# Attention followed by gated products on one core: places of two weight tiles, planner tables with PE's modes, and value products as one operation

## The chip, the cores and the metric
One NeuronCore of a Trainium2 chip runs the whole program. The metric is device microseconds of one execution; lower is better. TensorE is called PE below, VectorE DVE, ScalarE ACT, GpSimd POOL, SyncE SP.

## The reference
Inputs are q, k and v of 4 batches, 12 heads, 448 positions and 64 columns, and three weight matrices. In short:

```python
scores = q @ k.transpose / 8;  scores above the diagonal = -1e9
p = exp(scores - rowmax);  p = p / (p.sum + 1e-9)
x = (p @ v), heads side by side            # 1792 x 768
out = ((x @ w_a) * (x @ w_b)) @ w_out      # w_a, w_b 768 x 1536, w_out 1536 x 768
```

## The kernel before, in words
**Attention.** Two heads make a pair; there are 6 pairs a batch. For each pair `scores` (line 388) makes the lower triangle of q k in seven rows of blocks, r = 0 to 6, with 64x64 tiles of PE (line 413, four operations a pair: rows 6 and 5, row 0, rows 4 and 3, rows 2 and 1), takes each row's maximum on DVE (line 422) and its exponential on ACT (line 428), and scales by the inverse sum: on POOL for batches 0 and 1 (line 442), on ACT for batches 2 and 3 (line 441). `turn` (line 451) transposes p by PE in two turns of 8 (line 460), four to a PSUM bank (t0, t1), and copies each bank to SBUF on ACT or DVE. `values` (line 470) multiplies by v in 128x64 tiles of PE (line 478): four operations a pair, one for each quarter c of the keys, each of two products per head half; quarters 0 and 3 read the first turn, 1 and 2 the second. The result is x, split into a rounded part x_hi and a remainder x_lo (batches 0 and 1) or stored to HBM as x_keep (batches 2 and 3).

**Products.** Weights come in as 64-bit words, are made float32 in six steps (`convert_unit`, line 302) and split into w_hi (ACT) and w_lo (DVE). The tiles w_hi and w_lo have 18 slots of 128 x 128 each, 512 bytes a slot and partition. `products` (line 577) issues three matmuls of 448 columns for each 128-deep slice: w_hi by x_hi, w_hi by x_lo, w_lo by x_hi (line 581). Batches 0 and 1 go first: 24 units for a and b, 12 for the output. Batches 2 and 3 follow with seven products in place of eight (`seven`, line 658); `take_first` and `take_second` prepare their operands from x_keep. Attention of batches 2 and 3 is woven between the products of batches 0 and 1: one pair every 30 slices (`AT`, `attend`, line 762).

**Order.** Every operation is recorded with an engine and a duration (`Plan.op`, line 99), and its number is its urgency. `Plan.order` (line 123) then runs a clock per engine: at each step the engine that is free first takes the ready operation of the lowest number. When an operation is ready follows from the end of its predecessors plus `WAIT[engine][engine]` and `MARGIN`. What comes out is the order in which each engine executes; nothing is changed on the chip. Buffers are rings (`ring`, line 90): a new user of a slot waits for all users of the old one.

**Places.** Tiles are laid one behind the other in SBUF. Before, w_hi and w_lo start at 64 modulo 512 bytes in a partition, and the moving operands (x_hi, x_lo, g_hi, g_lo and the rooms of the second half) at 64 modulo 256, with slices of 1792 bytes, which is 7 times 256.

Of the kernel before, what the change touches and what calls it, by code (L numbers as in the profile page):

```python
# [79 lines left out]
class Plan:  # L80
# [18 lines left out]
    def op(self, engine, ns, fn, reads=(), writes=()):  # L99
# [21 lines left out]
        self.ops.append((engine, ns, fn, deps, self.soonest))  # L121

    def order(self):
# [16 lines left out]
        count = 0  # L140
        while count < n:
# [14 lines left out]
            if now[e]:  # L156
                i = now[e][0]
                limit = at + PATIENCE[e] * self.ops[i][1]
                first = [s for s in soon[e] if s[0] < limit and s[1] < i - GAP] if PATIENCE[e] else []
                if first:  # L160
                    s = min(first, key=lambda s: s[1])
                    soon[e].remove(s)
                    heapq.heapify(soon[e])
                    at, i = s
                else:
                    heapq.heappop(now[e])
            else:
                i = heapq.heappop(soon[e])[1]
# [7 lines left out]
            else:  # L176
                free[e] = end[i] = at + self.ops[i][1]
# [17 lines left out]
def pe_ns(n, passes=1):  # L195
    return max(passes * n / 2.4, 107.0) + 2.5
# [19 lines left out]
def causal_attention_then_gated_product(  # L216
# [39 lines left out]
    g_lo = const.tile([P, 2, HF, S], F32R, name="g_lo")  # L256
    w_keep = [dram.tile([P, UW], F32, name=f"w_keep{u}") for u in range(NU)]
# [44 lines left out]
    def convert_unit():  # L302
# [12 lines left out]
        plan.op("dve", 660, lambda: nc.vector.tensor_scalar(  # L315
            out=e.t, in0=high(), scalar1=0x7FF00000, scalar2=None, op0=ALU.bitwise_and), [t], [e])
        plan.op("dve", 660, lambda: nc.vector.tensor_scalar(
# [4 lines left out]
        plan.op("dve", 1030, lambda: nc.vector.scalar_tensor_tensor(  # L322
            out=r(), in0=m.t, scalar=2.0**32, in1=low(), op0=ALU.mult, op1=ALU.add), [m, t], [m])
        plan.op("dve", 1030, lambda: nc.vector.scalar_tensor_tensor(
            out=e.t, in0=high(), scalar=0x80000000, in1=e.t,
            op0=ALU.bitwise_and, op1=ALU.bitwise_or), [t, e], [e])
        plan.op("dve", 1030, lambda: nc.vector.scalar_tensor_tensor(  # L327
# [60 lines left out]
    def scores(b, hp):  # L388
        qk_t = qk.pop((b, hp))
        st = plan.ring("st", 2, None)  # L390
        st.tile = st_buf[nth[3] % 2]
# [7 lines left out]
        for part, tags in ((FIRST, ("s0", "s1")), (SECOND, ("m", "m") if b < 2 else ("t0", "t1"))):  # L399
            banks = [bank(tag, 3 if tag == "m" else 1) for tag in tags]  # L400
            at = {}
            for rs in part:
# [14 lines left out]
                plan.op("pe", pe_ns(D * (rs[0] + 1), 4) + 60, mm, [(qk_t, 0), (qk_t, 1)], [at[r][0] for r in rs])  # L417
            for r in [r for rs in part for r in rs]:
# [16 lines left out]
        plan.op("dve", 165, lambda: nc.vector.tensor_scalar_add(st.t[:, rc, 0:NR], st.t[:, sm, 0:NR], 1.0e-9),  # L435
                [(st, sm, r) for r in rows], [(st, rc, r) for r in rows])
        plan.op("dve", 170, lambda: nc.vector.reciprocal(st.t[:, rc, 0:NR], st.t[:, rc, 0:NR]), [], [(st, rc, r) for r in rows])
        for r in rows:
# [7 lines left out]
            ns = act_ns(D * (r + 1), False, 1) if NORM[b] == "act" else pool_ns(D * (r + 1))  # L446
# [23 lines left out]
    def values(b, hp, x):  # L470
        ps, vt = bank("pv"), v_of.pop((b, hp))
        parts = dict(pt)
        for c in range(4):
            n, (o, count) = next((n, g[1:]) for n in range(2) for g in groups[n] if g[0] == c)

            def mm(c=c, n=n, o=o, count=count):
                for j in range(2):
# [4 lines left out]
                return r  # L482
# [393 lines left out]
```

## Time and profile before

| | us |
|---|---|
| median of 3 runs (670.26 to 671.44) | 671.21 |
| the profiled execution | 670.64 |
| its span, first to last instruction | 668.9 |
| PE busy (3,956 matmuls) | 659.9 |
| DVE busy | 453.7 |
| ACT busy | 349.0 |
| POOL busy | 49.8 |

The span is cut below at 101.7 us, where the first long run of products begins, and at 387.1 us, where the last value products end. Durations of matmuls are modelled and overlap; how fast PE goes is read from the starts of instructions one behind the other.

### The profile page before, as it was taken

What the parts mean: (1) busy time and instruction counts of PE and PEld (TensorE: products, weight loads), DVE (VectorE), ACT (ScalarE), POOL (GpSimd) and SP (SyncE); (2) the same over time, 40 slices, a digit from 0 to 9 for tenths busy, and PEclk for the clock granted to TensorE, in tenths of its full rate; (3) what the DMA queues carried; (4) which work ended last, traced back from release to release, by engine and by line L of the source; (5) the groups of instructions that cost most, each with busy time, mean ns of one, the idle gap of its engine ahead of it and who ended that gap; (6) DMA issues with size and microseconds to landing.
All of it is one profiled execution on the core that took longest, in us unless ns stands there. A gap on an engine that the chain in (4) does not pass through costs nothing.

```text
span 668.9 us, 10897 instructions
## 1 busy us (share of the span) xinstructions
PE 659.9 (99%) x3956; PEld 559.8 (84%) x3956; DVE 453.7 (68%) x1005; ACT 349.0 (52%) x826; POOL 49.8 (7%) x104
## 2 busy tenths in 40 slices
PE   8999999999999999999999999999999999999997
PEld 6554469889888888888988989999999999999997
DVE  4778878888778567568768795588762237886431
ACT  5888746765675675675576742244432234443110
POOL 3546530000000000000000000000000000000000
PEclk9999999999999999999999999999999999999999
DMA  8535535666476665454432275212133232122532
GB/s 281 179 98 182 168 89 202 219 211 204 163 241 242 210 217 207 125 197 160 167 126 73 68 230 164 91 60 71 50 94 103 102 103 60 60 72 79 163 112 95
DMA packets 41717, 95.87 MB, mean 143 GB/s; under 512 B 4800, under 2 KB 27840, under 8 KB 41664
## 3 DMA queue, kind: packets, MB, share of 16 engines
q1 hardware_dynamic: 41664, 95.18, 43.3%
q8 instruction: 31, 0.51, 0.3%
q14 instruction: 22, 0.18, 0.1%
HBM read 67.24 MB, written 27.92 MB: 142 GB/s over the span
## 4 chain that ended last, share of the span: by engine, by line
PE 95%; POOL 3%; DVE 1%; POOLq 0%; issue 0%; ACT 0%
PE m L581 76%; PE t L460 7%; PE pv L478 5%; PE s L413 3%; POOL early L442 2%; PE t L413 2%; PE m L413 2%; POOL p L442 1%; PE fill L816 1%; POOLq L871 0%; DVE pt L272 0%; DVE p L422 0%; DVE w L327 0%; ACT w_hi L264 0%; DVE mid L280 0%
## 5 line engine op out<-in xcount | busy, mean ns | idle before, releaser
L581 PE MATMUL m<-x_hi,w_hi 128*128 128x448 f32 x432 | 161.2, 373 | 0.0
L581 PE MATMUL m<-x_hi,w_lo 128*128 128x448 f32 x432 | 157.9, 366 | 0.0
L581 PE MATMUL m<-x_lo,w_hi 128*128 128x448 f32 x432 | 157.8, 365 | 0.0
L280 DVE TENSOR_TENSOR w_lo<-w,w_hi 128x768 fp32r<-128x768 f32 (+1 forms) x84 | 66.0, 786 | 63.3 <-ACT w_hi L264 62.5
L581 PE MATMUL m<-g_hi,w_hi 128*128 128x448 f32 x288 | 106.1, 368 | 0.0
L581 PE MATMUL m<-g_hi,w_lo 128*128 128x448 f32 x288 | 105.3, 366 | 0.0
L581 PE MATMUL m<-g_lo,w_hi 128*128 128x448 f32 x288 | 105.3, 365 | 0.0
L264 ACT ACTIVATE w_hi<-w 128x768 fp32r<-128x768 f32 (+1 forms) x84 | 59.2, 705 | 71.0 <-PE m L581 49.3
L581 PEld LDWEIGHTS m<-x_hi,w_hi 128*128 128x128 f32 x432 | 81.3, 188 | 8.4 <-issue 1.7
L581 PEld LDWEIGHTS m<-x_hi,w_lo 128*128 128x128 f32 x432 | 81.1, 188 | 6.7
L581 PEld LDWEIGHTS m<-x_lo,w_hi 128*128 128x128 f32 x432 | 81.2, 188 | 6.1
L264 ACT ACTIVATE mid<-m 128x448 f32<-128x448 f32 x72 | 38.9, 540 | 90.4 <-PE m L581 76.8
L428 ACT ACTIVATE p<-p,st 128x384 f32<-128x384 f32 (+6 forms) x126 | 62.4, 497 | 23.8 <-DVE st L422 23.6
L280 DVE TENSOR_TENSOR mid<-m,acc 128x448 f32<-128x448 f32 x48 | 29.9, 624 | 46.3 <-PE m L581 45.6
L581 PEld LDWEIGHTS m<-g_hi,w_hi 128*128 128x128 f32 x288 | 54.1, 188 | 4.5
L581 PEld LDWEIGHTS m<-g_hi,w_lo 128*128 128x128 f32 x288 | 54.1, 188 | 4.4
L581 PEld LDWEIGHTS m<-g_lo,w_hi 128*128 128x128 f32 x288 | 54.1, 188 | 4.2
L264 ACT ACTIVATE pt<-t 128x512 f32<-128x512 f32 x72 | 40.6, 596 | 26.5 <-PE t L460 26.1
L478 PE MATMUL pv<-pt,v 128*64 128x448 f32 (+3 forms) x384 | 49.5, 389 | 0.0
L478 PEld LDWEIGHTS pv<-pt,v 128*64 128x64 f32 x384 | 24.5, 136 | 22.6 <-issue 11.5
L460 PE MATMUL t<-ident,p 128*128 128x128 f32 x180 | 38.8, 279 | 0.9 <-DVE pt L272 0.7
L280 DVE TENSOR_TENSOR mid<-m,mid 128x448 f32<-128x448 f32 x36 | 22.5, 625 | 23.5 <-PE m L581 23.2
(90 smaller groups left out, 999.2 us busy)
## 6 DMA issues: line engine op xcount, KB each, us to landing
w<-w SPq DMA_DIRECT2D x36, 768.0 KB, 4.5
w_keep<-w SPq DMA_DIRECT2D x36, 384.0 KB, 2.9
w<-w_keep SPq DMA_DIRECT2D x36, 384.0 KB, 3.1
raw<-qT SPq DMA_DIRECT2D x24, 224.0 KB, 2.6
raw<-kT SPq DMA_DIRECT2D x24, 224.0 KB, 3.1
o_keep<-mid SPq DMA_DIRECT2D x24, 224.0 KB, 2.0
acc<-o_keep SPq DMA_DIRECT2D x24, 224.0 KB, 2.7
out<-mid SPq DMA_DIRECT2D x24, 224.0 KB, 1.9
```

Source lines behind the costliest of these rows:

```text
L264: return nc.scalar.activation(o(), i(), AF.Copy)
L280: plan.op(engine, ns, lambda: e.tensor_tensor(out=o(), in0=a(), in1=b(), op=op), reads, writes)
L413: x = nc.tensor.matmul(at[r][0].t[to * D:(to + 1) * D, at[r][1]], q[:, r * D:(r + 1) * D], k[:, 0:D * (r + 1)], start=True, stop=True)
L428: return nc.scalar.activation(view(r), view(r), AF.Exp, bias=st.t[:, nm, r:r + 1], scale=-1.0, accum_out=st.t[:, sm, r:r + 1],)
L442: return nc.gpsimd.tensor_scalar(out=view(r), in0=view(r), scalar1=st.t[:, rc, r:r + 1], scalar2=1.0, op0=ALU.mult, op1=ALU.mult)
L460: return nc.tensor.matmul(t.t[:, P * i:P * (i + 1)], p.t[:, PO[r] + P * c:PO[r] + P * (c + 1)], swapped if r % 2 else ident, is_transpose= ...
L478: r = nc.tensor.matmul(ps.t[j * D:(j + 1) * D, 128 * c:S], vt.t[:, c, j, :], parts[n].t[:, j, o:o + count, :].rearrange("p i d -> p (i d)" ...
L581: r = nc.tensor.matmul(ps.t[:, :S], a[:, i, :], x(), start=first and n == 0, stop=last and n == 2, skip_group_check=part)
L816: plan.filler = lambda: nc.tensor.matmul(fill[:, 0:P], warm, warm, start=True, stop=True)
```

## The change
It has four parts. The two weight tiles move behind the other constant tiles, each behind a spacer of 192 bytes, so that w_hi starts at 0 modulo 512 and w_lo at 192 modulo 256. The planner's waits and durations are set anew, and PE's operations carry a mode: "q" for scores, "c" for values, "f" for all others. A change of mode is charged `SWITCH` nanoseconds on the plan's clock, and where the most urgent ready operation of PE is of another mode, PE takes the first ready one of the mode at hand if its number is less than `NEAR` = 100 beyond. The four operations of `values` become one, which reads both turns' copies and both parts of v. The ring of small tiles st, which hold a pair's maxima and sums, goes from 2 to 4 slots.

```diff
 WAIT = {
-    "pe": {"pe": 0, "act": 200, "dve": 200, "pool": 270, "sp": 200},
-    "act": {"pe": 260, "act": 140, "dve": 145, "pool": 205, "sp": 150},
-    "dve": {"pe": 290, "act": 130, "dve": 130, "pool": 205, "sp": 150},
-    "pool": {"pe": 260, "act": 320, "dve": 320, "pool": 200, "sp": 250},
+    "pe": {"pe": 0, "act": 180, "dve": 210, "pool": 270, "sp": 200},
+    "act": {"pe": 160, "act": 140, "dve": 110, "pool": 205, "sp": 150},
+    "dve": {"pe": 150, "act": 100, "dve": 130, "pool": 210, "sp": 150},
+    "pool": {"pe": 80, "act": 200, "dve": 200, "pool": 200, "sp": 250},
...
-MARGIN = 60
+MARGIN = 20
+NEAR = 100
+SWITCH = {"fq": 95, "qf": 160, "qc": 220, "cq": 220, "fc": 150, "cf": 107}
...
             if now[e]:
                 i = now[e][0]
+                if e == "pe" and self.ops[i][5] != mode:
+                    alike = [j for j in now[e] if self.ops[j][5] == mode and j < i + NEAR]
+                    if alike:
+                        i = min(alike)
...
-                free[e] = end[i] = at + self.ops[i][1]
+                ns = self.ops[i][1]
+                if e == "pe":
+                    ns += SWITCH.get(mode + self.ops[i][5], 0)
+                    mode = self.ops[i][5]
+                free[e] = end[i] = at + ns
...
-    st_buf = [sbuf.tile([P, 3, 8], F32, tag=f"st{i}", name=f"st{i}") for i in range(2)]
+    st_all = sbuf.tile([P, 4, 28], F32, tag="st", name="st")
+    st_buf = [st_all[:, i, 0:24].rearrange("p (n r) -> p n r", n=3) for i in range(4)]
...
-    w_hi = const.tile([P, 18, P], F32R, name="w_hi")
-    w_lo = const.tile([P, 18, P], F32R, name="w_lo")
     v_buf = [const.tile([P, 4, 2, D], F32, name=f"v{i}") for i in range(NVB)]
...
     g_lo = const.tile([P, 2, HF, S], F32R, name="g_lo")
+    const.tile([P, 48], F32, name="space")
+    w_hi = const.tile([P, 18, P], F32R, name="w_hi")
+    const.tile([P, 48], F32, name="space_2")
+    w_lo = const.tile([P, 18, P], F32R, name="w_lo")
...
-        plan.op("dve", 660, lambda: nc.vector.tensor_scalar(
+        plan.op("dve", 470, lambda: nc.vector.tensor_scalar(
...
-        plan.op("dve", 1030, lambda: nc.vector.scalar_tensor_tensor(
+        plan.op("dve", 900, lambda: nc.vector.scalar_tensor_tensor(
...
-    st = plan.ring("st", 2, None)
+    st = plan.ring("st", 4, None)
...
-                plan.op("pe", pe_ns(D * (rs[0] + 1), 4) + 60, mm, [(qk_t, 0), (qk_t, 1)], [at[r][0] for r in rs])
+                plan.op("pe", pe_ns(D * (rs[0] + 1), 4), mm, [(qk_t, 0), (qk_t, 1)], [at[r][0] for r in rs], "q")
...
-                plan.op("dve", dve_ns(n) + 70, negmax, [at[r][0], "mask"], [(p, r), (st, nm, r)])
-                plan.op("act", act_ns(n, False, 3), exp, [(st, nm, r)], [(p, r), (st, sm, r)])
+                plan.op("dve", dve_ns(n) + 10, negmax, [at[r][0], "mask"], [(p, r), (st, nm, r)])
+                plan.op("act", act_ns(n, False, 2), exp, [(st, nm, r)], [(p, r), (st, sm, r)])
...
-            ns = act_ns(D * (r + 1), False, 1) if NORM[b] == "act" else pool_ns(D * (r + 1))
+            ns = act_ns(D * (r + 1)) if NORM[b] == "act" else pool_ns(D * (r + 1))
...
-        for c in range(4):
-            n, (o, count) = next((n, g[1:]) for n in range(2) for g in groups[n] if g[0] == c)
-
-            def mm(c=c, n=n, o=o, count=count):
+        def mm():
+            for c in range(4):
+                n, (o, count) = next((n, g[1:]) for n in range(2) for g in groups[n] if g[0] == c)
                 for j in range(2):
...
-            plan.op("pe", pe_ns(S - 128 * c, 4) + 60, mm,
-                    [(vt, 1 if c == 3 else 0), (parts[n], 0), (parts[n], 1)], [ps])
+        plan.op("pe", sum(pe_ns(S - 128 * c, 4) for c in range(4)), mm,
+                [(vt, 0), (vt, 1), *((parts[n], h) for n in range(2) for h in range(2))], [ps], "c")
```

## Rows read from the trace of the kernel before

**Rows 1.** The page: PE's sum, granted clock by slice, and the chain's shares.
```profile
PE 659.9 (99%) x3956; PEld 559.8 (84%) x3956; DVE 453.7 (68%) x1005; ACT 349.0 (52%) x826; POOL 49.8 (7%) x104
...
PEclk9999999999999999999999999999999999999999
...
PE 95%; POOL 3%; DVE 1%; POOLq 0%; issue 0%; ACT 0%
```

**Rows 2.** Busy time (and count) by stage: all engines, then PE and weight loads of line 581.
```profile
0.00:101.70 101.70, 96.47 (x820) 56.91 (x820) 75.19 (x270) 71.56 (x220) 49.79 (x104) 1.00 0.52 167
...
387.10:668.90 281.80, 278.04 (x1371) 257.38 (x1371) 1.00 0.32 101
...
0.00:668.90 668.90, 515.87 (x2484) 463.33 (x2484) 1.00 0.44 143
```

**Rows 3.** Timeline, products stage: start us, duration us, engine, what, count.
```profile
387.01 0.47 PE L581 MATMUL m<-g_hi,w_hi 128*128 128x448 f32 x1
...
599.92 0.36 PE L581 MATMUL m<-x_hi,w_hi 128*128 128x448 f32 x1
...
600.32 0.37 PE L581 MATMUL m<-x_hi,w_lo 128*128 128x448 f32 x1
600.53 0.36 PE L581 MATMUL m<-x_hi,w_hi 128*128 128x448 f32 x1
...
601.13 0.36 PE L581 MATMUL m<-w_x,w_hi 128*128 128x448 f32 x1
...
664.77 0.37 PE L581 MATMUL m<-g_hi,w_lo 128*128 128x448 f32 x1
```

**Rows 4.** Timeline of PE, attention stage, values of one pair and scores of another.
```profile
43.29 0.97 PE L478 MATMUL pv<-pt,v 128*64 128x448 f32 x4
44.20 0.33 PE L460 MATMUL t<-ident,p 128*128 128x128 f32 x1
...
45.59 0.33 PE L460 MATMUL t<-swapped,p 128*128 128x128 f32 x1
45.75 0.27 PE L460 MATMUL t<-ident,p 128*128 128x128 f32 x1
45.86 0.27 PE L460 MATMUL t<-swapped,p 128*128 128x128 f32 x1
46.06 0.97 PE L413 MATMUL s<-raw 64*64 64x448 f32 x8
46.96 0.33 PE L460 MATMUL t<-ident,p 128*128 128x128 f32 x1
...
47.33 0.27 PE L413 MATMUL s<-raw 64*64 64x64 f32 x2
```

**Rows 5.** Timeline of PE, mixed stage, one pair.
```profile
120.30 0.36 PE L581 MATMUL m<-x_hi,w_lo 128*128 128x448 f32 x1
120.59 1.02 PE L413 MATMUL s<-raw 64*64 64x448 f32 x10
...
122.47 1.95 PE L478 MATMUL pv<-pt,v 128*64 128x448 f32 x16
124.34 0.47 PE L581 MATMUL m<-x_hi,w_hi 128*128 128x448 f32 x1
```

**Rows 6.** Timeline of PE, attention stage: a transpose that waits for a copy.
```profile
15.87 0.27 PE L460 MATMUL t<-swapped,p 128*128 128x128 f32 x1
16.82 0.44 PE L460 MATMUL t<-ident,p 128*128 128x128 f32 x2 [0.68 <-DVE pt L272]
```

**Rows 7.** Timeline of DVE, then of PE, where the second half begins.
```profile
402.56 0.62 DVE L280 TENSOR_TENSOR w_x<-raw,pt_x 128x448 fp32r<-128x448 f32 x1
...
424.21 0.36 PE L581 MATMUL m<-x_hi,w_hi 128*128 128x448 f32 x1
```

**Rows 8.** What PE waited for to 101.7 us: sum us, times, longest us.
```profile
PE t L460 <- POOL early L442: 2.2, 4, 0.7
PE t L460 <- POOL p L442: 1.0, 3, 0.6
```

More of the change, by code (lines that the diff above doesn't have):

```diff
@@ L97, in ring, with op @@
         return slots[i]
-    def op(self, engine, ns, fn, reads=(), writes=()):
+    def op(self, engine, ns, fn, reads=(), writes=(), mode="f"):
         i, deps = len(self.ops), set()
@@ L120, in op @@
         deps.discard(i)
-        self.ops.append((engine, ns, fn, deps, self.soonest))
+        self.ops.append((engine, ns, fn, deps, self.soonest, mode))
     def order(self):
@@ L139, in order @@
         out = []
-        count = 0
+        count, mode = 0, "f"
         while count < n:
@@ L165, in order @@
                 else:
-                    heapq.heappop(now[e])
+                    now[e].remove(i)
+                    heapq.heapify(now[e])
             else:
@@ L313, in r @@
             return m.t.bitcast(F32)
-        plan.op("dve", 660, lambda: nc.vector.tensor_scalar(
+        plan.op("dve", 470, lambda: nc.vector.tensor_scalar(
             out=e.t, in0=high(), scalar1=0x7FF00000, scalar2=None, op0=ALU.bitwise_and), [t], [e])
-        plan.op("dve", 660, lambda: nc.vector.tensor_scalar(
+        plan.op("dve", 470, lambda: nc.vector.tensor_scalar(
             out=m.t, in0=high(), scalar1=0x000FFFFF, scalar2=0x00100000,
@@ L321, in convert_unit @@
             e.t, e.t, AF.Copy, bias=-896.0 * 2**23, scale=8.0), [e], [e])
-        plan.op("dve", 1030, lambda: nc.vector.scalar_tensor_tensor(
+        plan.op("dve", 900, lambda: nc.vector.scalar_tensor_tensor(
             out=r(), in0=m.t, scalar=2.0**32, in1=low(), op0=ALU.mult, op1=ALU.add), [m, t], [m])
-        plan.op("dve", 1030, lambda: nc.vector.scalar_tensor_tensor(
+        plan.op("dve", 900, lambda: nc.vector.scalar_tensor_tensor(
             out=e.t, in0=high(), scalar=0x80000000, in1=e.t,
             op0=ALU.bitwise_and, op1=ALU.bitwise_or), [t, e], [e])
-        plan.op("dve", 1030, lambda: nc.vector.scalar_tensor_tensor(
+        plan.op("dve", 900, lambda: nc.vector.scalar_tensor_tensor(
             out=wt.t, in0=r(), scalar=2.0**-52, in1=e.t.bitcast(F32),
@@ L389, in scores @@
         qk_t = qk.pop((b, hp))
-        st = plan.ring("st", 2, None)
-        st.tile = st_buf[nth[3] % 2]
+        st = plan.ring("st", 4, None)
+        st.tile = st_buf[nth[3] % 4]
         nth[3] += 1
@@ L430, in exp @@
                     )
-                plan.op("dve", dve_ns(n) + 70, negmax, [at[r][0], "mask"], [(p, r), (st, nm, r)])
-                plan.op("act", act_ns(n, False, 3), exp, [(st, nm, r)], [(p, r), (st, sm, r)])
+                plan.op("dve", dve_ns(n) + 10, negmax, [at[r][0], "mask"], [(p, r), (st, nm, r)])
+                plan.op("act", act_ns(n, False, 2), exp, [(st, nm, r)], [(p, r), (st, sm, r)])
         rows = range(NR)
-        plan.op("dve", 165, lambda: nc.vector.tensor_scalar_add(st.t[:, rc, 0:NR], st.t[:, sm, 0:NR], 1.0e-9),
+        plan.op("dve", 76, lambda: nc.vector.tensor_scalar_add(st.t[:, rc, 0:NR], st.t[:, sm, 0:NR], 1.0e-9),
                 [(st, sm, r) for r in rows], [(st, rc, r) for r in rows])
-        plan.op("dve", 170, lambda: nc.vector.reciprocal(st.t[:, rc, 0:NR], st.t[:, rc, 0:NR]), [], [(st, rc, r) for r in rows])
+        plan.op("dve", 122, lambda: nc.vector.reciprocal(st.t[:, rc, 0:NR], st.t[:, rc, 0:NR]), [], [(st, rc, r) for r in rows])
         for r in rows:
```

2 lines of the change are left out of this document (1 added, 1 removed).

## The prediction

> **What bounds the kernel now.** Four views, in this order. The page's sums come first: TensorE (PE) is busy 659.9 us of a span of 668.9, and the clock granted to it is at its upper level (2.4 GHz) in all forty slices [rows 1]. A busy PE is not by itself PE at its peak, so the chain of waits is next: 95% of the path that ended last is PE, and POOL has 3% [rows 1]. Third, the span cut in three [rows 2]: an attention stage up to 101.7 us (VectorE, DVE, 75.2 us busy, ScalarE, ACT, 71.6), a mixed stage up to 387.1 us with attention of batches 2 and 3 between products, and a stage of products alone. Last the timeline of PE, to see the pace inside each stage.
>
> In the products stage nothing waits. Its 1,371 matmuls [rows 2] start from 387.01 to 664.77 us [rows 3]: 277.76 / 1,370 = 0.2027 us each. 448 columns at 2.4 GHz are 0.1867 us, so each costs 0.016 us more than its columns. All 2,484 products [rows 2] therefore hold 2,484 x 0.2027 = 503.5 us, three quarters of the span, and only two things shorten the rest: fewer matmuls, which the change doesn't bring, or a shorter step.
>
> In the attention stage PE goes to and fro between three kinds of work: transposes and products (f), score products of 64x64 tiles (q), value products of 128x64 tiles (c). The reader is to see in [rows 4] that the value products of one pair fall into two stretches with a transpose between, and that transposes break the scores of one pair as well; in [rows 5], from the mixed stage, both lie in one stretch each. By the whole timeline of PE to 101.7 us I count 31 stretches of q for 13 pairs and 23 of c for 12 pairs, 18 and 11 more than one a pair.
>
> **The price of going to and fro.** Values: whole, from 122.47 to 124.34 = 1.87 us [rows 5]; broken, from 43.29 to 45.59 = 2.30 with one transpose in it [rows 4]. A transpose among transposes takes 0.11 (45.75 to 45.86) [rows 4], so the break costs 2.30 - 1.87 - 0.11 = 0.32. The transposes' side of such a break is the two between scores (46.96 to 47.33), which take 0.37 and not 0.22: 0.15 of it [rows 4]. The other half is the way back into the tiled mode to the tiles, which scores pay as values do. I take 0.30 us for a further round trip, of values or of scores.
>
> **Value products as one operation.** The instructions stay (16 matmuls a pair); three waits and three places where the planner may put other work go. All 11 breaks go: 11 x 0.30 = 3.3 us. What it adds is a wait: the first quarter now also waits for the copies of the second turn. Behind the waiting matmul nothing on PE can pass, and the split of the result into x (ACT, DVE) comes later, which nobody needs before the products. The price of one such wait when nothing lies between: last transpose at 15.87, then DVE's copy out of the bank, and the next transpose into it at 16.82 [rows 6]; 0.95 - 0.11 = 0.84 us. Over 12 pairs the ends are 0 and 10.1 us. I take 1.0, near the lower end, because scores of the next pair, which need none of these copies, can lie between: as they do at 46.06 behind three transposes [rows 4].
>
> **PE's mode in the planner.** It stays with the kind of work at hand while an operation of that kind, ahead of or less than 100 numbers behind the most urgent one, is ready. Score products of one pair need no other engine's work between them, so most of the 18 further stretches can go; the PSUM banks that wait for VectorE's reads hold some. I take 13 of 18: 13 x 0.30 = 3.9 us (ends 0 and 18 x 0.30 = 5.4). In the mixed stage each pair has one stretch of each already [rows 5], so nothing is gained. There the rule lets products go ahead of ready scores, for up to 100 numbers. By the code a pair's share of the stage is 30 product operations, 35 that bring weights in and results out, and 57 of attention, 122 numbers in (387.1 - 101.7) / 12 = 23.8 us, so 100 are about 20 us. Values of the last pair feed the second half; its preparation ends on DVE at 402.56 + 0.62 and PE reads the first of it at 424.21 [rows 7]: 21 us of cover. I cost it at nothing; beyond the cover it costs a us for each us.
>
> **Tables and st.** Waits and durations change the plan's guesses, not the work. PE waits for POOL 3.2 us in the attention stage as the trace names it [rows 8], so better guesses are worth 0 to 3.2 there, and nothing later, where PE has no wait; an order that is rebuilt can lose as much. I take 0; what hides any other shift is the queue of ready work ahead of PE. Two more st slots take away a wait of DVE for POOL's norms two pairs back, off PE's path: 0, and the same 3.2 if PE's waits come from there.
>
> **The places of w_hi and w_lo.** All tiles that PE reads start now at 64 modulo 256 bytes and step by multiples of 256, so no row shows any other phase. Slices of x lie in turn at 64 and 320 modulo 512, yet two slices in turn take 0.61 and 0.60 us for their three products (599.92, 600.53, 601.13) [rows 3]: a step of 256 does nothing. So bounds: at best a product takes its columns alone, 0.016 x 2,484 = 39.7 us less. Nearer is how close the value products come to their columns: 1,024 columns in four passes at 2.4 GHz are 1.707 us of their 1.87 [rows 5]; a way out of a mode costs 0.09 of that (transpose to scores, 45.86 to 46.06, 0.20 in place of 0.11 [rows 4]), and 0.07 over eight steps leaves 0.009 each. By that a product could take 0.196: 0.0067 x 2,484 = 16.6 us less. The last product ahead of a switch, which has no weight load beside it, takes 120.30 to 120.59 = 0.29 [rows 5], 0.20 without the way out: 0.0027 x 2,484 = 6.7 us less. On the other side, a single start told to a hundredth can lie 0.21 behind the one before (600.32 to 600.53) [rows 3]; 0.21 throughout is 0.0073 x 2,484 = 18 us more. I take 0, the row that is there. The Trainium skill has a rule against this part (TensorE: Matmul & The Clock Gate, Step-by-step: what each phase is for): PE has two SBUF read ports, so that loading weights steals nothing from a running matmul. By it the places change nothing and the sum stays; that a product with a load beside it takes 0.203 and one without 0.20 doesn't settle it.
>
> **Sum.** Profiled execution 670.64 us (span 668.9 and 1.7 around it). -3.3 - 3.9 + 1.0 = -6.2: 664.4. The median of the runs is 0.57 above the profiled one: 671.2 - 6.2 = 665.0. DVE and ACT are busy 75.2 and 71.6 of 101.7 us in the attention stage [rows 2], so the gain isn't stopped by them.
>
> **Rivals.** (A) The new phase shortens the products' step, to 0.200: 658.3; to 0.196: 648.4; to its columns: 625. For it: 0.016 us a step are unexplained, and a step without a load beside it is shorter by the rows. Against: no row at another phase, and the 0.20 is told to a hundredth only. 0.27. The Trainium skill (TensorE: Matmul & The Clock Gate, Back-to-back issue gap) puts the gap of a warm stream at the columns plus 2.5 ns; by it, an estimate, a product could take 0.189 and A's end would be 631, where the trace has 0.203. (B) The switches go, but chains through POOL's norms and the copies take their place as waits of PE: 3.2 us of such waits are there already [rows 8], and PE's path has POOL in it. Gain of about 1.5: 669.7. 0.15. (C) Slower: the wait ahead of the merged value products. It decides when it is uncovered in more than 7.2 / 0.84 = 9 of 12 pairs; in all of them, 10.1 - 7.2 = +2.9: 674.1. For it: none of the 2,484 products can start before x of batch 0 is whole. Against: scores usually are. 0.07. (D) A worse phase, up to 18 less 6.2: 683. 0.05. The forecast has 0.46.
>
> **How the numbers follow.** The forecast with its bounds spans 661 to 669; A reaches down; I stop at 651, between 0.200 and 0.196, which leaves out the lower third of A (0.09), and at 672, which leaves out most of C and D (0.09). 0.2% (1.3 us) is about what a measurement of this kernel can tell from no change. Faster by more: the forecast, A and half of B, 0.81; within: most of the rest of B and a little of C, 0.08; slower: 0.11.
>
> **What would show it.** Right: 12 unbroken stretches of values and under 20 of scores before the products begin, an attention stage some 6 us shorter, and a step of 0.2027 as before. Wrong: a product step that moves at all (A or D; then weight loads or starts show it in the last stage at once); idle PE ahead of each pair's values (C); as many round trips as before, or fewer with PE waiting for POOL (B); idle PE near 424 us, where the cover of 21 us ends.

## Result and the profile after

The median fell from 671.07 us (670.26 to 671.44, 4 runs) to 658.84 us (658.08 to 659.52, 4 runs): a ratio of 0.9819, 95% interval 0.9802 to 0.9836, a gain of 12.2 us. The forecast was 6.2. The profiled execution took 658.89 us, its span 657.1.

The page of the kernel after, which answers [rows 1]: PE's sum, the granted clock, the chain's shares.

```profile
PE 650.0 (99%) x3956; PEld 560.7 (85%) x3956; DVE 452.7 (69%) x1005; ACT 347.6 (53%) x826; POOL 49.7 (8%) x104
...
PEclk9999999999999999999999999999999999999999
...
PE 86%; DVE 7%; ACT 6%; issue 0%; POOLq 0%; POOL 0%; ACTq 0%
```

The instructions are as many as before and the clock is at its upper level (2.4 GHz) throughout, so nothing of the gain is the clock's. PE is still the bound, though its share of the chain is 86% and not 95%: POOL has gone from it, and DVE (7%) and ACT (6%) have come in.

Stages of the kernel after, cut at the first product behind the front's last values and at the first product of the last stage: length, PE's busy time and count. First all instructions of the front, then products alone (line 596, which was 581).

```profile
0.00:96.54 96.54, 93.44 (x846) 65.03 (x846) 79.14 (x274) 70.19 (x216) 49.74 (x104) 1.00 0.59 186
...
0.00:96.54 96.54, 15.25 (x66) 11.88 (x66) 1.00 0.59 186
96.54:393.88 297.34, 242.18 (x1122) 206.88 (x1122) 1.00 0.52 178
393.88:657.10 263.22, 259.47 (x1296) 243.22 (x1296) 1.00 0.31 94
```

The same cuts in the trace of before:

```profile
0.00:101.64 101.64, 9.63 (x39) 6.97 (x40) 1.00 0.52 167
101.64:387.01 285.37, 228.11 (x1074) 198.90 (x1074) 1.00 0.52 177
```

The front is 5.1 us shorter although 66 products were done in it and not 39. To compare kernels that place products differently, I take 0.200 us off for each product in a stage, and call what remains the stage's rest (the front is the stretch up to the first cut, the mixed stage the one up to the second): 101.6 - 7.8 = 93.8 before, 96.5 - 13.2 = 83.3 after. The mixed stage's rest went from 285.4 - 214.8 = 70.6 to 297.3 - 224.4 = 72.9.

First and last product of the last stage, which answers [rows 3] (start, duration, engine and line):

```profile
393.89 0.47 PE L596 MATMUL m<-g_hi,w_hi 128*128 128x448 f32 x1
...
653.00 0.36 PE L596 MATMUL m<-g_hi,w_lo 128*128 128x448 f32 x1
```

259.11 / 1,295 = 0.2001 us a product, where it was 0.2027. So the step moved, and so did the order. In the front, scores and values now lie whole:

```profile
23.57 1.08 PE L428 MATMUL s<-raw 64*64 64x448 f32 x12
24.59 1.95 PE L493 MATMUL pv<-pt,v 128*64 128x448 f32 x16
26.47 0.33 PE L475 MATMUL t<-ident,early 128*128 128x128 f32 x1
```

The sixteen value products take 24.59 to 26.47, 1.88 us, as whole ones did in the mixed stage of before [rows 5]; the broken ones took 2.30 [rows 4]. Up to the front's last values there are 12 stretches of values (23 before) and 18 of scores (31 before). What PE waited for in the front, of which [rows 8] had 3.2 us of POOL:

```profile
PE t L475 <- POOL early L457: 0.8, 1, 0.8
PE t L475 <- ACT pt L279: 0.5, 1, 0.5
PE t L475 <- POOL p L457: 0.4, 2, 0.2
```

### The profile page after: what moved, and what is told of

It reads as the page before. It is cut to its first block, busy times and chain, and to the rows that moved or that the text cites. A ratio compares the mean times of both kernels' runs of the same rounds, so it can differ in the third digit from the quotient of the medians.

```text
span 657.1 us, 10875 instructions
## 1 busy us (share of the span) xinstructions
PE 650.0 (99%) x3956; PEld 560.7 (85%) x3956; DVE 452.7 (69%) x1005; ACT 347.6 (53%) x826; POOL 49.7 (8%) x104
## 4 chain that ended last, share of the span: by engine, by line
PE 86%; DVE 7%; ACT 6%; issue 0%; POOLq 0%; POOL 0%; ACTq 0%
PE m L596 72%; PE t L475 5%; PE pv L493 4%; ACT p L443 3%; PE s L428 2%; PE t L428 1%; DVE early L437 1%; DVE pt L287 1%; ACT p L456 1%; PE fill L831 1%; DVE p L437 1%; PE m L428 1%; DVE w_lo L295 1%; DVE w_m L337 1%; DVE w_e L339 1%
## 5 line engine op out<-in xcount | busy, mean ns | idle before, releaser
L443 ACT ACTIVATE p<-p,st 128x448 f32<-128x448 f32 (+6 forms) x126 | 62.4, 497 | 24.7 <-DVE st L437 24.7
L493 PE MATMUL pv<-pt,v 128*64 128x448 f32 (+3 forms) x384 | 46.8, 386 | 0.0
L335 ACT ACTIVATE w_e<-w_e 128x768 uint32<-128x768 uint32 x36 | 30.3, 841 | 26.5 <-DVE w_e L330 26.3
L279 ACT ACTIVATE g_hi<-mid 128x448 fp32r<-128x448 f32 x48 | 27.6, 574 | 27.1 <-DVE mid L295 26.9
```

Of the source, the lines that this page charges most:

```text
L279: return nc.scalar.activation(o(), i(), AF.Copy)
L335: plan.op("act", 840, lambda: nc.scalar.activation(e.t, e.t, AF.Copy, bias=-896.0 * 2**23, scale=8.0), [e], [e])
L443: return nc.scalar.activation(view(r), view(r), AF.Exp, bias=st.t[:, nm, r:r + 1], scale=-1.0, accum_out=st.t[:, sm, r:r + 1],)
L493: r = nc.tensor.matmul(ps.t[j * D:(j + 1) * D, 128 * c:S], vt.t[:, c, j, :], parts[n].t[:, j, o:o + count, :].rearrange("p i d -> p (i d)" ...
```

## Experiments

Two theories stood at first. The prediction's: the order is worth 6.2 us and the places nothing. Its rival A: the places shorten the step to 0.200. Each part was put alone on the kernel before, and each was taken out of the kernel after.

**Places alone, and all but the places.**

```diff
-    w_hi = const.tile([P, 18, P], F32R, name="w_hi")
-    w_lo = const.tile([P, 18, P], F32R, name="w_lo")
...
+    const.tile([P, 112], F32, name="space")
+    w_hi = const.tile([P, 18, P], F32R, name="w_hi")
+    const.tile([P, 48], F32, name="space_2")
+    w_lo = const.tile([P, 18, P], F32R, name="w_lo")
```

> The kernel before with the two weight tiles moved alone: w_hi at 0 modulo 512 and w_lo at 192 modulo 256, order and all other places as before. If the places shorten the products' step: 0.2002 us as in the changed kernel, 2,484 x 0.0025 = 6.2 us less, 664.9. If the shorter step comes from anything else (the shift of the other tiles by 256, the order): 0.2027 and 671.1.

> The changed kernel with both weight tiles put back to 64 modulo 512, everything else as changed. If places and order are two gains that add: step 0.2027, 658.8 + 6.2 = 665.0, the median that was forecast. If the order needs the faster step, or the step doesn't hang on the places: 671 or 658.8.

Places alone: 666.83 us (666.35 to 667.09), ratio 0.9934 (0.9918 to 0.9951), 4.4 us less with the order untouched. All but the places: 661.99 (661.74 to 662.25), ratio 0.9863 (0.9848 to 0.9877): the order is worth 9.2 us at the old places, and the places 3.2 on the new order. So places do count, but neither 0.200 nor 0.2027 came out everywhere. Last stage with the places alone:

```profile
383.69 0.47 PE L583 MATMUL m<-g_hi,w_hi 128*128 128x448 f32 x1
...
660.84 0.37 PE L583 MATMUL m<-g_hi,w_lo 128*128 128x448 f32 x1
```

277.15 / 1,370 = 0.2023, at weight and moving tiles with the same starts modulo 256 as in the kernel after, which has 0.2001. The start alone doesn't tell the step.

**Values as one operation alone; the rule and its charges alone**, each on the kernel before.

> The kernel before with the value products as one operation and nothing else. If each of the 11 breaks costs 0.30 us and the wait for the last copies is covered: 12 stretches of values before the products, 3.3 - 1.0 = 2.3 us less, 668.8. If the wait is uncovered in all 12 pairs: 10.1 - 3.3 = 6.8 us more, 677.9.

> The kernel before with the modes of PE in the planner (the charge for a change and the choice of an operation of the mode at hand) and nothing else. If score products stay together for lack of other causes: some 18 stretches of scores in place of 31 and 3.9 us less, 667.2. If what they wait for keeps them apart or comes back as waits of PE: 671.1.

664.35 us (663.72 to 665.16), ratio 0.9898 (0.9884 to 0.9913), and 665.29 (663.71 to 666.52), ratio 0.9910 (0.9895 to 0.9926). Both are more than forecast, and the sum, 12.7, is more than the 9.2 of all order parts together. The mean step of the mixed stage differed too (203.8 ns before, 202.9 and 203.3 here, over the distances between neighbouring products), so these two can't be read as prices of the order alone; the last two runs below can.

**Tables alone, and the kernel after with the old tables** (waits between engines, margin and durations).

> The kernel before with the tables alone (waits between engines, margin, durations); two st slots, no mode rule, values in four operations, weights where they were. Theory 'tables are worth nothing': 671.1, within 1 us. Rival 'the tables carry part of the order's 9.2 us': values alone gave 6.8 and the mode rule alone 5.9, 12.7 in sum where all the order parts together gave 9.2; if the tables add on top they show as a gain of 2 us or more here (669 or less), and if they are what eats 3.5 us of the sum they show as a loss (674).

> The kernel after with the old tables (waits, margin, durations); mode rule, charges, values as one, four st slots and places as in after. Theory 'tables are worth nothing': 658.8, within 1 us. Rival 'values and rule need the tables to place the switches where buffers are free': 661 or more. Rival 'the tables eat part of the gain': 656 or less.

671.45 us (670.50 to 674.15, 10 runs), ratio 1.0014 (1.0003 to 1.0025), and 658.05 (657.99 to 659.59), against 658.84 for the kernel after. In the whole time the tables are worth nothing that can be told, as forecast; neither was tried at places where the step has one value. The stages tell more. The front's rest of the kernel after is 83.3 us, with the old tables 84.5; its mixed stage's rest is 72.9, with the old tables 70.9. More on that below. Of the tables alone the profiled execution was the slowest, 674.15, and its last stage shows why:

```profile
385.06 0.47 PE L581 MATMUL m<-g_hi,w_hi 128*128 128x448 f32 x1
...
668.29 0.37 PE L581 MATMUL m<-g_hi,w_lo 128*128 128x448 f32 x1
```

283.23 / 1,370 = 0.2067 with the weights where before has 0.2027.

**The step by the weights' starts.** Streams of products alone, 60 for each pair of starts, the weight tiles sliced out of a longer one:

```python
hi = w_hi[:, 16 * a + P * slot:16 * a + P * (slot + 1)]
lo = w_lo[:, 16 * b + P * slot:16 * b + P * (slot + 1)]
```

> Only streams of products (448 columns, triples hi by x_hi, hi by x_lo, lo by x_hi) with nothing beside them; the attention, the real weights and all results are left out, so its time is read stream by stream. 64 streams of 60 products, one for each pair of starts of the hi and lo weight tiles (steps of 64 bytes over 512), each behind two small fp32 matmuls. Theory 'the address sets the step': hi and lo both at 64 modulo 512, as before, give 0.2027 us a product, hi at 0 and lo at 192 modulo 256 give 0.200, each stream keeps one mean from its first dozen products on, and the pairs fall into a table of a few values. Rival 'the step locks to a phase that the last change of mode leaves': streams with the same addresses modulo 256 differ from each other by as much as streams with different ones (0.200 to 0.2027), and the mean can change within a stream. Rival 'contention with the other engines' traffic': with nothing beside PE all 64 pairs give one step, below 0.2027.

One stream, hi at 0 and lo at 64: its second and its last product.

```profile
26.73 0.36 PE L54 MATMUL m<-x_lo,w_hi 128*128 128x448 f32 x1
...
38.58 0.36 PE L55 MATMUL m<-x_hi,w_lo 128*128 128x448 f32 x1
```

11.85 / 58 = 0.2043. The mean distance over the last 30 products of each stream, in ns, rows by w_hi's start and columns by w_lo's, both modulo 256, moving tiles at 64:

```
            lo 0    lo 64   lo 128  lo 192
hi 0       200.0   204.4   199.9   200.1
hi 64      202.2   202.7   204.4   202.1
hi 128     204.4   202.2   202.3   203.2
hi 192     202.2   205.4   201.8   203.8
```

The 48 streams whose starts differ from these by 256 repeat the table within 0.2, but for two cells: with lo at 320, hi at 64 gives 206.7 (202.7 above), and with lo at 256, hi at 128 gives 202.1 (204.4 above). With no other engine at work the starts make 3% of a product (199.9 to 206.7), so contention with the rest of the kernel is not the cause; yet two cells have two values.

**The same with the moving tiles' start as a third axis** (`x_hi[:, 16 * x + k * S:...]`).

> Streams of products alone again (attention, real weights and results left out); 64 streams, one for each start of the moving tiles (0, 64, 128, 192 modulo 256) by hi weights by lo weights (the same four). In the kernels and in the first table the moving tiles start at 64. Theory 'what counts is the weight tile's start against the moving tile's': the table moves with the moving tile, so that moving tiles at 0 give for hi at 192 what moving tiles at 64 give for hi at 0 (200.0), and hi at 0 is no longer the best row. Rival 'the weight tile's own start counts': the row of hi at 0 stays at 200.0 to 200.3 in all four quarters and the row of 64 at 202 or above. A step below 200.0 anywhere would show a better place: 2484 products by each ns is 2.5 us.

The low row moves with the moving tiles: it is hi at 192 for moving tiles at 0, at 0 for 64, at 64 for 128 and at 128 for 192 (settled means 199.9 to 200.1, and 204.4 to 204.5 where lo starts where the moving tiles do). What counts is the start of the weights against that of the moving tile: w_hi 64 bytes below it modulo 256, w_lo anywhere but at the same start. No pair came below 199.9. Steps under 64 bytes weren't tried.

**Does the way in choose the step?** Eight pairs, each entered in eight ways:

```diff
+                if c:
+                    nc.tensor.matmul(m[2][:, :S - 56 * (c - 1)], w_hi[:, 16 * a:16 * a + P], x_hi[:, 0, :S - 56 * (c - 1)],
+                                     start=True, stop=True)
```

> Streams of products alone, as in the run before (attention, real weights and results left out). Eight pairs of weight starts (hi, lo modulo 512: 64 and 64, 0 and 192, 0 and 0, 0 and 128, 0 and 64, 64 and 0, 128 and 128, 192 and 192), each entered in eight ways: straight behind the two small fp32 matmuls, or behind one more fp32r product of 448, 392, 336, 280, 224, 168 or 112 columns. Theory 'lock': a pair has a few steps, and the entry chooses: 64 and 64 gives 202.67 in some streams and about 206.6 in others (both were seen: 202.67 in before, 206.66 in the last stage of the kernel with the tables alone), 0 and 192 gives 200.0 in most and 202.22 in some (as in the last stage of the kernel with the places alone). Rival 'the address alone': all eight streams of a pair agree within 0.3 ns, and what the kernels with the same addresses differ by comes from the other engines' traffic.

The pair of the kernel after, 0 and 192, entered straight behind the small products, then behind one more product of 448 columns (second product of the stream and its last):

```profile
116.42 0.36 PE L57 MATMUL m<-x_lo,w_hi 128*128 128x448 f32 x1
...
128.15 0.37 PE L58 MATMUL m<-x_hi,w_lo 128*128 128x448 f32 x1
...
129.02 0.36 PE L56 MATMUL m<-x_hi,w_hi 128*128 128x448 f32 x1
...
140.82 0.36 PE L58 MATMUL m<-x_hi,w_lo 128*128 128x448 f32 x1
```

11.73 / 58 = 0.2022 and 11.80 / 59 = 0.2000, from the same addresses. And the pair of the kernel before, behind one more product of 448 columns and behind one of 392:

```profile
26.62 0.36 PE L56 MATMUL m<-x_hi,w_hi 128*128 128x448 f32 x1
...
38.58 0.37 PE L58 MATMUL m<-x_hi,w_lo 128*128 128x448 f32 x1
...
39.42 0.36 PE L56 MATMUL m<-x_hi,w_hi 128*128 128x448 f32 x1
...
51.61 0.37 PE L58 MATMUL m<-x_hi,w_lo 128*128 128x448 f32 x1
```

11.96 / 59 = 0.2027 and 12.19 / 59 = 0.2066. Settled values by entry: 0 and 192 end at 200.0 in four and at 202.2 in four; 64 and 64 at 202.7 in six and 206.7 in two; 0 and 128 at 200.0 in two and 204.4 to 204.5 in six; 0 and 0 at 200.0 in all eight. Of the other four, 64 and 0 has two values as well (202.2 in seven, 204.4 in one), 128 and 128 (202.2) and 192 and 192 (204.0) have one, and 0 and 64 ends at 201.0 to 201.3 in all eight, where the two runs before gave 204.4. So a stream locks to one of a few steps: the starts set which there are, and the way in has a part in which of them it gets. It isn't the whole of it, since 0 and 64, entered straight, gave one value in the first run and another here. The two values that the kernels showed at each place are the two of this table.

**Without the rule, twice, and with the rule in the front alone.** The charges for a switch stay in the plan.

```diff
-                if e == "pe" and self.ops[i][5] != mode:
+                if False:
```

```diff
+FRONT = 88e3
...
-                if e == "pe" and self.ops[i][5] != mode:
+                if e == "pe" and at < FRONT and self.ops[i][5] != mode:
```

> The kernel after without the rule that stays in a mode (the charges for a switch stay in the plan); values as one operation, tables, st slots and places as in after. Theory 'the parts overlap: values as one takes most of the round trips, the rule those that remain in the front': about 661.2 (671.1 less 6.8 for values and 3.15 for the places), so the rule is worth 2.4 us on top. Rival 'the rule pays nothing once values are one operation, since what it saves ahead of 95 us it gives back in the mixed stage': 658.8, no difference. Rival 'the rule costs': below 658.8, the best of all so far.

> The kernel after without the rule that stays in a mode, once more with more rounds, since its four runs spread from 655.8 to 660.0. Theory 'the rule costs in the mixed stage what it saves in the front, and more' (non-product time of the front 83.7 against 81.3, of the mixed stage 68.1 against 72.6): 656.8, about 2 us less than after. Rival 'its streams lock now and then to a worse step': the runs fall into two groups, 656 and 660, and the median is that of after, 658.8.

> The kernel after with the rule only while the plan's clock is under 88 us (the front's twelve values operations are planned by then); past that, the order by age as in the kernel before, the charges kept. Theory 'the rule saves 2.4 us in the front and costs 4.5 in the mixed stage': front 81 us and mixed stage 68 us beside the products, so 654.3 to 655, below both the kernel after and the one without the rule. Rival 'what the front saves comes back as a later wait in the mixed stage': 656.8 or more, with a mixed stage of 70 us or more beside its products.

Without the rule 656.98 us (655.78 to 659.99) and, again, 657.86 (656.28 to 659.42); with the rule in the front alone 655.69 (654.96 to 658.44), ratio 0.9784 (0.9765 to 0.9802). All three medians lie below that of the kernel after (658.84), as if the rule cost more in the mixed stage than it saves in the front; but the runs spread too far to tell. The four runs of the second set fall into two groups, 656.28 and 656.66, 659.06 and 659.42, 3 us apart. That is the lock again; last stage of the profiled execution of each set:

```profile
375.78 0.48 PE L596 MATMUL m<-g_hi,w_hi 128*128 128x448 f32 x1
...
649.90 0.36 PE L596 MATMUL m<-g_hi,w_lo 128*128 128x448 f32 x1
```

```profile
376.03 0.47 PE L596 MATMUL m<-g_hi,w_hi 128*128 128x448 f32 x1
...
653.18 0.37 PE L596 MATMUL m<-g_hi,w_lo 128*128 128x448 f32 x1
```

One kernel, two executions (on two chips, but the groups stand within one set): 274.12 / 1,370 = 0.2001 and 277.15 / 1,370 = 0.2023, 3.0 us apart.

**Both weights at 0 modulo 256.** If the entry chooses, the pair with one step must end the spread.

```diff
-    const.tile([P, 48], F32, name="space_2")
     w_lo = const.tile([P, 18, P], F32R, name="w_lo")
+    const.tile([P, 48], F32, name="space_2")
```

> The kernel after with w_lo at 0 modulo 256 instead of 192, nothing else. In the streams alone the pair 0 and 192 ended at 200.0 in four entries and at 202.23 in the other four; the pair 0 and 0 at 200.0 in all eight. Theory 'the entry chooses the step': the last stage stays at 200.0, the mixed stage falls from 201.98 to about 200.3 (992 products: 1.7 us less), so 657.2, with runs within 1 us of each other. Rival 'the two places are alike in the kernel': 658.8 and a mixed stage at 202.

> The rule in the front only, and w_lo at 0 modulo 256. The profiled run of the kernel with the front rule and w_lo at 192 took 657.18 with a last stage at 202.22 (1369 products) and a mixed stage at 201.86 (973). Theory 'the entry chooses': 200.0 and 200.3 in their place take 3.0 and 1.5 us off: 652.6, runs within 1 us. Rival 'the two places are alike in the kernel': runs between 655 and 658.4 as before, median 655.7.

> The kernel before with both weights at 0 modulo 256 (w_hi and w_lo at 0 modulo 512) and the order untouched. With 0 and 192 the order of before took 666.83, its last stage locked at 202.22 and its mixed stage at 200.79. Theory 'the entry chooses': 200.0 in the last stage, 200.3 in the mixed one, 3.0 and 0.5 us less: 663.3, so the places are worth 7.8 us of the 671.1 where the entry can't spoil them. Rival 'the other engines' traffic set the 202.22': 666.8.

> The last kernel with two st slots instead of four. Theory of the prediction 'the slots are never waited for': no difference to it, within 0.5 us. Rival 'four slots let the next score stretch's maxima start before the one before the last is normalised': slower by 1 us or more, with more time ahead of the last values operation of the front.

The kernel after so changed: 657.00 us (656.82 to 657.60), ratio 0.9797 (0.9784 to 0.9810). With the rule in the front alone: 653.59 (653.05 to 653.72), ratio 0.9743 (0.9730 to 0.9756), 5.2 us below the kernel after and the best of all. The order of before: 663.04 (662.55 to 663.31), ratio 0.9885 (0.9871 to 0.9898), where 0 and 192 gave 666.83. All three came within 1.0 us of what the lock theory expected, the last stage of each at 0.2001, and their runs lie within 0.8 us. Two st slots in place of four: 654.32 (653.89 to 654.53), ratio 0.9755 (0.9741 to 0.9768), 0.7 us above the four of the best kernel. The intervals of the two ratios overlap, but no run with four slots took longer than 653.72 and none with two less than 653.89.

**The order's parts where the step has one value.** The two edits of before, again, with both weights at 0.

> Order of before with the values of a pair as one operation, and both weights at 0 modulo 256, so that the step is 200.0 and no lock disturbs the comparison with the 663.04 of before's order at these places. Theory of the prediction '11 breaks of 0.30 us each': 659.7. Rival 'a break inside a pair's values also holds waits for copies' (the streams between the values of one pair cost 5 us in the trace of before): 658 or less, with the front some 5 us shorter beside its products and the mixed stage unchanged at 68.

> Order of before with the mode rule and the charges alone, both weights at 0 modulo 256. Theory of the prediction '13 fewer score stretches of 0.30 us, nothing in the mixed stage': 659.1. Rival 'the front gains more and the mixed stage pays': a front some 5 us shorter beside its products, a mixed stage 4 us or more longer, 661 to 662.

Values as one: 657.73 us (657.23 to 658.18), 5.3 below 663.04. The rule with its charges: 658.54 (658.19 to 659.23), 4.5 below. Stages of before's order, values as one, and the rule, all at 0 and 0 (front with all of PE's work, then products alone in front and mixed stage):

```profile
0.00:100.90 100.90, 95.74 (x819) 56.22 (x820) 75.09 (x270) 71.51 (x220) 49.74 (x104) 1.00 0.52 168
...
0.00:100.90 100.90, 9.64 (x39) 6.97 (x40) 1.00 0.52 168
100.90:382.56 281.66, 224.41 (x1074) 198.61 (x1074) 1.00 0.52 179
```

```profile
0.00:97.72 97.72, 93.92 (x825) 60.27 (x825) 76.25 (x270) 70.47 (x220) 46.70 (x104) 1.00 0.54 172
...
0.00:97.72 97.72, 10.81 (x45) 7.92 (x45) 1.00 0.54 172
97.72:378.20 280.48, 223.47 (x1068) 197.43 (x1068) 1.00 0.52 180
```

```profile
0.00:101.53 101.53, 97.34 (x862) 65.15 (x862) 81.26 (x281) 73.33 (x223) 47.06 (x104) 1.00 0.56 181
...
0.00:101.53 101.53, 15.14 (x66) 11.84 (x66) 1.00 0.56 181
101.53:393.71 292.18, 241.94 (x1122) 204.63 (x1123) 1.00 0.54 180
```

All order parts (the kernel after at 0 and 0), and the same with the rule in the front alone, of which the mixed stage:

```profile
0.00:96.18 96.18, 92.71 (x846) 64.48 (x846) 79.17 (x274) 70.22 (x216) 49.97 (x104) 1.00 0.58 187
...
0.00:96.18 96.18, 15.27 (x66) 11.89 (x66) 1.00 0.58 187
96.18:391.96 295.78, 240.50 (x1122) 206.47 (x1122) 1.00 0.52 179
```

```profile
96.37:373.71 277.34, 219.33 (x1047) 193.48 (x1047) 1.00 0.52 178
```

With the products taken off as above (us; PE idle is the length less PE's busy time; the mixed rest of the last line is 277.34 - 209.4):

| both weights at 0 | front's rest | of it PE idle | mixed rest | median |
|---|---|---|---|---|
| order of before | 93.1 | 5.2 | 66.9 | 663.04 |
| values as one | 88.7 | 3.8 | 66.9 | 657.73 |
| rule and charges | 88.3 | 4.2 | 67.8 | 658.54 |
| all, as in after | 83.0 | 3.5 | 71.4 | 657.00 |
| all, rule in the front | 83.2 | 3.1 | 67.9 | 653.59 |

The start of an execution varies: the first score begins at 4.88 us in the trace of the first line, at 5.05 in that of the fourth and at 5.61 or 5.62 in the other three (one kernel, that without the rule, had 5.29 and 5.62 in its two executions). With these 0.2 to 0.7 us taken off the later fronts the stages add up to the medians within 0.3 us. So values as one operation gain 5.1 us in the front and nothing in the mixed stage, the outcome of that run's rival and not of the 3.3; the rule alone gains 5.5 and pays 0.9.

The order of after takes 10.1 us out of the front and puts 4.5 into the mixed stage, of which 3.5 go when the rule stops at the front. The rule alone put only 0.9 into the mixed stage, so it is dear there together with the other parts. How the order changes is seen in the kernel after, between one pair's scores and its transposes:

```profile
149.96 1.02 PE L428 MATMUL s<-raw 64*64 64x448 f32 x10
...
158.03 0.27 PE L475 MATMUL t<-ident,p 128*128 128x128 f32 x1
158.14 0.27 PE L475 MATMUL t<-swapped,p 128*128 128x128 f32 x1
...
159.92 0.27 PE L475 MATMUL t<-swapped,p 128*128 128x128 f32 x1
```

Between a pair's last transposes and the next scores there now stand 54 to 63 products (84 ahead of the first), where 6 or 9 stood before, so scores come late and the transposes only 8.1 us behind them (158.03 - 149.96). Before, they came 19 us behind (scores at 120.59 [rows 5], transposes at 139.7) and lay in eights. Now they lie mostly in ones to fours with products between.

That they are broken is not what costs. A product behind a transpose starts 0.03 us after it and the next product 0.29 after that: 0.32, where a transpose (0.11) and a product (0.20) take 0.31. And the rule alone, on the old tables, breaks them more often: in its mixed stage a product follows a transpose 66 times, in that of all parts 53 times, in the order of before 25 times, and yet it pays 0.9 us and not 4.5 (its mixed stage has 12 scores less, some 0.7 us at 0.06 each). What costs is that the transposes wait. The last pair of the mixed stage with all parts at 0 and 0, first PE, then the chain of work around it:

```profile
372.60 0.27 PE L475 MATMUL t<-swapped,p 128*128 128x128 f32 x1
372.84 0.33 PE L475 MATMUL t<-ident,p 128*128 128x128 f32 x1
373.24 0.33 PE L475 MATMUL t<-swapped,p 128*128 128x128 f32 x1
```

```profile
371.80 1.40 ACT p L456 x4
373.20 0.04 issue
373.24 0.33 PE t L475
```

Three transposes that would take 0.11 each start 0.24 and 0.40 us apart, the last when ACT's normalisation of p (line 456) has ended. The distances from one transpose to the next in the mixed stage, and how late the products right behind transposes start (us; over 0.109 for a transpose behind a transpose, over 0.028 for a product behind one):

| mixed stage | distances | of them above 0.125 | all together over 0.109 each | products late by | mixed rest |
|---|---|---|---|---|---|
| order of before, 0 and 0 | 167 | 0 | 0.0 | 0.0 | 66.9 |
| rule and charges, 0 and 0 | 126 | 2 | 0.1 | 0.0 | 67.8 |
| all, 0 and 0 | 139 | 33 | 2.7 | 0.9 | 71.4 |
| all, rule in the front, 0 and 0 | 167 | 8 | 0.4 | 0.0 | 67.9 |
| kernel after, 0 and 192 | 139 | 32 | 2.6 | 0.9 | 72.9 |
| kernel after with the old tables, 0 and 192 | 127 | 2 | 0.1 | 0.0 | 70.9 |

Of the 2.7 us with all parts the trace names ACT's normalisation of p for 1.7 and ACT's copies for 0.5. With all parts these waits come to 3.6 us, which is the 3.5 that the rule costs in the mixed stage (653.59 and 657.00 put it at 3.4). The last two lines differ in the tables alone: with the old ones the same rule puts a product behind a transpose 65 times, and hardly a transpose behind another starts late (transposes behind products are 2.1 us late in sum, not 0.5, and 1.6 of it is one wait for ACT's copy; so the mixed stage gains 2.0 and not 3.5). The old tables put 320 ns between the end of an ACT operation and an operation of PE that needs it (260 and the margin of 60), the new ones 180 (160 and 20). So it is the rule with the new tables that puts transposes into the order before their p is ready; which of the tables' numbers does it wasn't tried. Of the 1.0 that stays when the rule stops at the front, 0.4 lies in such distances and 0.4 in one transpose that waits for ACT's copy (at 107.6 us).

## Why the prediction was wrong, point by point

**What bounds the kernel.** Right. PE is the bound in every kernel, and the two things in which the prediction looked for time, round trips in the front and the product's step, are the two that moved. Its share of the chain fell from 95 to 86%, though, and in the mixed stage PE did come to wait.

**The places, taken at 0.** This is the step that failed, and most of the miss. The chosen row, slices of x at 64 and 320 modulo 512 with the same time [rows 3], was true and told nothing: but for two cells the table repeats every 256 bytes. No row showed another start, and I took the one that was there, with the price of a change as a rival of 0.27. Rival A named the change and its size: 0.200 in place of 0.2027, 658.3; the last stage went to 0.2001 and the time to 658.84. That the time fits so well is in part luck, as what follows shows. At places with one step the same order fell by 7.9 us (670.94 to 663.04); A's 2,484 x 0.0027 = 6.7 leaves out that before's mixed stage had a mean of 203.8 ns, between the two steps of its places (202.7 and 206.7). In the kernel after only part of that comes: its mixed stage had a mean of 202.0 ns, again between its two, and moving w_lo to 0 took off 1.8 more. D's worse phase exists as well (64 and 128: 204.4; 64 and 64 itself has 206.7), but the change went the other way. The Trainium skill's rule that was weighed against this part (TensorE: Matmul & The Clock Gate, Step-by-step: what each phase is for: two read ports, so a weight load steals nothing from a running matmul) didn't bear out as "places are free": with nothing but products running, the weights' start moved the step from 199.9 to 206.7 ns. Its gap of 2.5 ns over the columns (the same page, Back-to-back issue gap, where the formula is called that of a single matmul by itself), by which an estimate gave 0.189, was reached by no pair; 0.200 was the least.

**Values as one operation, 3.3 less 1.0.** Stretches as predicted, 12 unbroken. PE's work in the front beside its products fell from 95.74 - 7.8 = 87.9 to 93.92 - 9.0 = 84.9: 3.0 us for 11 breaks, 0.27 each against 0.30, or 3.8 and 0.34 with the later start (5.62 against 4.88 us) taken off. The wait of 1.0 was wrong in sign: PE's idle time fell by 1.4 us, and of the waits that the trace names those for POOL fell from 3.2 to 1.6. So this term was too small: 2.3 forecast, 5.3 measured by the medians at 0 and 0. Rival C had no part.

**The rule, 3.9 in the front and nothing after.** Scores fell from 31 stretches to 18, in the kernel after and at both places, as the 13 of 18 had it. Alone the rule left 19, and 19 of values where 23 were: 16 fewer. It took 87.9 - (97.34 - 13.2) = 3.8 us of PE's work out of the front and 1.0 of idle time. The 3.8 meets the forecast's 3.9 by luck: the start was 0.7 us later, and the front held 796 matmuls beside the products and not 780. With values as one, work fell by 8.4 and idle time by 1.7: 24 stretches fewer, 0.35 each. The nothing of the mixed stage failed: 21 us of cover were counted behind the last values and they were there (the last stage shows no gap: 1,296 products at 0.2001), but the price was not at that end. It was paid at once: with the new tables, transposes came into the order before ACT was done with their p, and the waits cost 3.4 us. This term, taken at nothing, is the second step that failed.

**Tables and st, 0.** Right for the tables in the sum only (658.05 with the old ones, 658.84 with the new): "nothing later" failed, since under the rule they bring the mixed stage's waits, and the front gains about as much. The two more st slots were worth 0.7 us (653.59 against 654.32), and the front's rest is 1.4 us shorter with them (83.2 against 84.6): a small gain, not the 0.

**The sum.** At one step throughout the order is worth 663.04 - 657.00 = 6.0, and the forecast had 6.2. That is no merit of it: the front gave 10.1 and not 6.2, the mixed stage took 4.5 and not 0. At the old places it measured 9.2; the mixed stage's step differs between the two orders there (203.8 and 203.0), which is about 1 of the 3 us between, and the rest is not traced. So, counted at one step, the gain of 12.2 is 6 of order and 6 of step, and the second half was forecast at 0. The range, which had been drawn down to 651 for A's sake, holds the time.

**Rival B.** PE's waits for POOL fell from 3.2 to 1.2 us, with 0.5 for ACT beside them; the switches weren't replaced by waits in the front. In the mixed stage, where B wasn't looked for, waits for ACT did come.

## What to carry to other kernels

Where one instruction form makes up most of the span and takes more than its columns, look at the byte at which its operands start, modulo 256, before judging any other change, and put them where the step has one value, or differences of 3 us between orders and even between executions will be read as effects of the order. A row taken at one value of a parameter says nothing of another: if no row shows the changed place, the price is open, and streams of the instruction alone over all places tell it, if each is entered in several ways. A rule that batches like work should be let go where the engine is never short of work: it starts the chain of the other engines late, and with a plan that counts on their results too early the engine ends up waiting for them. Two changes that measure nothing and little each alone (the tables, the rule in the mixed stage) can cost together, so a term of 0 is to be checked stage by stage with the other parts in.

## What the runs showed of the hardware

- A stream of 448-column fp32r products, each with a weight load of 128 columns, has a step between 199.9 and 206.7 ns at the same granted clock (1.00, the 2.4 GHz level). It depends on the starts of the weights against those of the moving tile, modulo 256 bytes (tried in steps of 64); least, 199.9 to 200.1, with w_hi 64 bytes below the moving tile and w_lo not on the moving tile's start.
- The same addresses can hold two steps (200.0 and 202.2, 202.7 and 206.7, 200.0 and 204.4), and a stream keeps the one that it entered with: 1,370 products at 0.2001 in one execution and 0.2023 in the next of one kernel. Why there are such steps no run shows.
- A further stretch of another tile shape cost PE about 0.35 us of work in the front (8.4 us over 24; 3.0 over 11, or 3.8 with the later start taken off), besides the waits that it moves.
- Products put between two transposes cost next to nothing beyond their own time: 0.03 and 0.29 us where 0.11 and 0.20 stood, 0.32 against 0.31.
